# Chunked attention and a swish MLP on one core: blocks by batch, with crossbar and TensorE transposes, and the two products of a block in turn

## The chip, the cores and the metric

The kernel runs on one core of one Trainium2 chip. The metric is the device time of one execution in microseconds, as the median of several executions. Each run also lists the span of its instructions and the mean clock that the throttle granted to TensorE.

In this text PE is TensorE, PEld its weight loads, DVE is VectorE, ACT is ScalarE, POOL is GpSimd, and SP is SyncE, which here only issues DMAs.

## The reference

```python
def _attn_ref(q, k, v):                       # 8 batches, 8 heads, 576 tokens, 64 values each
    chunk, scale = 64, 1 / np.sqrt(64)        # attention inside chunks of 64 tokens only
    # q_c, k_c, v_c: reshaped to (B, H, 9, 64, 64)
    scores = scale * np.matmul(q_c, k_c.transpose(0, 1, 2, 4, 3))
    attn = softmax(scores)                    # cut
    return np.matmul(attn, v_c)               # reshaped back

def reference(q, k, v, w_in, w_out, beta):
    x = attn_out.transpose(0, 2, 1, 3).reshape(4608, 512)
    h = x @ w_in                              # 512 -> 2048, "first product"
    g = h * (1 / (1 + np.exp(-beta * h)))
    return g @ w_out                          # 2048 -> 512, "second product"
```

Both kernels compute in bf16 with f32 accumulation. They work on nine blocks of 512 tokens. A block has 64 matmuls of 128x512 in its first product and 64 in its second, 1152 "big" matmuls in all. Scores need q and k with the head dimension in the partitions, and the first product needs x with the model dimension in the partitions, so all three have to be transposed.

## The kernel before

Both kernels put every operation into the program order of its engine by a schedule of times, and waits on semaphores are worked out from what each operation reads and writes. This is also true of SP: in its program a DMA that has to wait stands before all DMAs scheduled later, even if those could go at once.

```python
def transpose_qk(blk, name, hp):              # 8 of these per block, 32x32 blocks, on VectorE
    P.op("dve", lambda e: e.transpose(
        tT[:, s, 4*hp:4*hp+4, :].rearrange("p g (t i) -> p i g t", i=4),
        ct[:, :, 2*hp:2*hp+2, :].rearrange("p i h d -> p i (h d)")), ...)

def scores(blk):                              # 128 matmuls of K=32, M=64, N=64
    ... e.matmul(A[64*hb:64*hb+64, m, col:col+64], kT[r, s, g, t], qT[r, s, g, t],
                 start=(dh == 0), stop=(dh == 1))

def transpose_x(blk, m, bank):                # 4 TensorE transposes, then a ScalarE copy
    ...
# ... loads, casts (POOL), exp (ACT), attend (PE), normalize (DVE) cut ...

for blk in range(NB):
    for n in range(16):                       # first product of blk beside second of blk - 1
        at(16 * blk + n, mm1, blk, n, bank)
        at(16 * (blk + 1) + n + 0.5, mm2, blk, n // 4, n % 4, 2 + (n // 4) % 2)
```

The softmax here doesn't subtract the row's maximum and nothing guards it: scores larger than these inputs give would overflow.

Of the kernel before, what the change touches and what calls it, by code (L numbers as in the profile page):

```python
# [6 lines left out]
ALU = mybir.AluOpType  # L7
# [9 lines left out]
class Program:  # L17
# [23 lines left out]
    def _depend(self, op, reads, writes):  # L41
# [17 lines left out]
        for key, v in writes:  # L59
            add(self.writer.get(key), op["queue"] == "pool")  # L60
            for r in self.readers.get(key, ()):
                add(r, False)
        for key, v in reads:
            self.readers.setdefault(key, []).append(op)
        for key, v in writes:
            self.writer[key] = op
            self.version[key] = v
            self.readers[key] = []
# [89 lines left out]
def bass_chunk_attention__then__act_swish_beta_kernel(nc, q, k, v, w_in, w_out, beta, out):  # L158
    B, H, S, D = q.shape
    NTOK = B * S  # L160
# [3 lines left out]
    NB = NTOK // 512  # L164
    CPB = S // 64

    with ExitStack() as es:
# [6 lines left out]
        beta_raw = sb("beta_raw", [128, NT], F32)  # L174
        beta_half = sb("beta_half", [128, NT], F32)
        w_in_bf = sb("w_in_bf", [128, NC, DFF], BF16)
        w_out_bf = sb("w_out_bf", [128, NT, 512], BF16)
        NWS = 4
        wstage = sb("wstage", [128, NWS, 2048], F32)
        NQS, NVS = 2, 2  # L180
        qstage = sb("qstage", [128, NQS, H, 256], F32)
        kstage = sb("kstage", [128, NQS, H, 256], F32)
        vstage = sb("vstage", [128, NVS, 4, 8, 64], F32)
        qcast = sb("qcast", [128, 4, H, 64], BF16)
        kcast = sb("kcast", [128, 4, H, 64], BF16)
        NQT = 2
        qT = sb("qT", [128, NQT, 2 * H, 128], BF16)
        kT = sb("kT", [128, NQT, 2 * H, 128], BF16)
        NVA = 2
        vaug = sb("vaug", [128, NVA, 8, 4, 66], BF16)  # L190
        E = sb("E", [128, 4, 512], BF16)
        rden = sb("rden", [128, 2, 2, 4], F32)
        x_sb = sb("x_sb", [128, 2, 512], BF16)
        NXT = 3
        xT = sb("xT", [128, NXT, NC, 512], BF16)
        tt = sb("tt", [128, 3, 512], BF16)
        g2 = sb("g2", [128, 2, NT, 512], BF16)
        NOS = 3
# [3 lines left out]
        F = es.enter_context(nc.psum_tensor("F", [128, 4, 512], F32))  # L202

        def chunk_runs(blk):
            g, end, runs = 8 * blk, 8 * blk + 8, []
            while g < end:
                b, c = divmod(g, CPB)
                n = min(end - g, CPB - c)
                runs.append((b, c, n, g - 8 * blk))
                g += n  # L210
            return runs


        def make_identity():
            P.op("pool", lambda e: e.memset(identity[:, :], 1.0), writes=[K("identity")])
            P.op("pool", lambda e: e.affine_select(
                out=identity[:, :], in_=identity[:, :], compare_op=ALU.is_equal, fill=0.0,
                base=0, pattern=[[-1, 128]], channel_multiplier=1),
                reads=[K("identity")], writes=[K("identity")])
            for s in range(NVA):  # L220
                P.op("pool", lambda e, s=s: e.memset(vaug[:, s, :, :, 64:65], 1.0),
                     writes=[K("vaug", s)])

        def load_beta():
            def f(e):
                with nc.allow_non_contiguous_dma(reason="beta is tiny"):
                    return e.dma_start(beta_raw[:, :], beta.rearrange("(t p) -> p t", p=128))
            P.dma("act", f, writes=[K("beta_raw")])
            P.op("dve", lambda e: e.tensor_single_scalar(
                beta_half[:, :], beta_raw[:, :], 0.5, ALU.mult),  # L230
# [3 lines left out]
        def load_qk(blk):  # L234
            s = blk % NQS
            for name, src, st in (("q", q, qstage), ("k", k, kstage)):
                for b, c, n, at in chunk_runs(blk):
                    def f(e, src=src, st=st, b=b, c=c, n=n, at=at):
                        a = src[b][:, 64 * c:64 * (c + n), :]
                        return e.dma_start(st[16 * at:16 * (at + n), s, :, :],  # L240
                                           a.rearrange("h (p i) d -> p h (i d)", i=4))
                    P.dma("sp", f, writes=[K(name + "stage", s, at, v=blk)])

        def load_v(blk):
            s = blk % NVS
            for b, c, n, at in chunk_runs(blk):
                for h in range(H):
                    def f(e, b=b, c=c, n=n, at=at, h=h):
                        a = v[b, h][64 * c:64 * (c + n), :]
                        r = 64 * (h % 2)  # L250
                        return e.dma_start(vstage[r:r + 64, s, h // 2, at:at + n, :],  # L251
                                           a.rearrange("(c j) d -> j c d", j=64))
                    P.dma("sp", f, writes=[K("vstage", s, at, h, v=blk)])

        def load_w_in(j):
            s = j % NWS

            def f(e):
                a = w_in[:, 512 * j:512 * (j + 1)].rearrange("(c p) f -> p c f", p=128)
                return e.dma_start(wstage[:, s, :].rearrange("p (c f) -> p c f", c=4), a)  # L260
            P.dma("sp", f, writes=[K("wstage", s, v=j)])

        def load_w_out(j):
            s = (4 + j) % NWS

            def f(e):
                a = w_out[512 * j:512 * (j + 1), :].rearrange("(t p) d -> p t d", p=128)
                return e.dma_start(wstage[:, s, :].rearrange("p (t d) -> p t d", t=4), a)
            P.dma("sp", f, writes=[K("wstage", s, v=4 + j)])

        def cast_w_in(j, engines):
            s = j % NWS
            for c, eng in enumerate(engines):
                dst = w_in_bf[:, c, 512 * j:512 * (j + 1)]
                src = wstage[:, s, 512 * c:512 * (c + 1)]
                if eng == "act":
                    P.op("act", lambda e, d=dst, a=src: e.activation(d, a, AF.Copy),  # L277
                         reads=[K("wstage", s, v=j)], writes=[K("w_in", j, c)])
                else:
                    P.op(eng, lambda e, d=dst, a=src: e.tensor_copy(d, a),  # L280
                         reads=[K("wstage", s, v=j)], writes=[K("w_in", j, c)])

        def cast_w_out(j, engines):
            s = (4 + j) % NWS
            for i, eng in enumerate(engines):
                dst = w_out_bf[:, 4 * j + i, :]
                src = wstage[:, s, 512 * i:512 * (i + 1)]
                if eng == "act":
                    P.op("act", lambda e, d=dst, a=src: e.activation(d, a, AF.Copy, scale=0.5),
                         reads=[K("wstage", s, v=4 + j)], writes=[K("w_out", 4 * j + i)])  # L290
                else:
                    P.op(eng, lambda e, d=dst, a=src: e.tensor_single_scalar(d, a, 0.5, ALU.mult),  # L292
                         reads=[K("wstage", s, v=4 + j)], writes=[K("w_out", 4 * j + i)])


        def stage_keys(name, blk):
            s = blk % NQS
            return [K(name + "stage", s, at, v=blk) for _, _, _, at in chunk_runs(blk)]

        def cast_qk(blk, name, eng):  # L300
            st, ct = (qstage, qcast) if name == "q" else (kstage, kcast)
            s = blk % NQS
            P.op(eng, lambda e: e.tensor_copy(  # L303
                ct[:, :, :, :].rearrange("p i h d -> p h i d"),
                st[:, s, :, :].rearrange("p h (i d) -> p h i d", i=4)),
                reads=stage_keys(name, blk), writes=[K(name + "cast", v=blk)])

        def transpose_qk(blk, name, hp):
            ct, tT = (qcast, qT) if name == "q" else (kcast, kT)
            s = blk % NQT  # L310
            P.op("dve", lambda e: e.transpose(  # L311
                tT[:, s, 4 * hp:4 * hp + 4, :].rearrange("p g (t i) -> p i g t", i=4),
                ct[:, :, 2 * hp:2 * hp + 2, :].rearrange("p i h d -> p i (h d)")),
                reads=[K(name + "cast", v=blk)], writes=[K(name + "T", s, hp, v=blk)])

        def cast_v(blk, eng, hp):
            s, sa = blk % NVS, blk % NVA
            keys = [K("vstage", s, at, h, v=blk) for _, _, _, at in chunk_runs(blk)
                    for h in (2 * hp, 2 * hp + 1)]
            P.op(eng, lambda e: e.tensor_copy(vaug[:, sa, :, hp, 0:64], vstage[:, s, hp, :, :]),  # L320
                 reads=keys, writes=[K("vaug", sa, hp, v=blk)])

        def scores(blk):
            s = blk % NQT
            for c2 in range(2):
                for hp in range(4):
                    for dh in range(2):
# [186 lines left out]
```

## Time and profile before

| | before |
|---|---|
| time, first median | 417.93 us |
| span of the profiled execution | 412.8 us |
| mean granted clock | 0.897 |
| steady block | about 41 us |
| big matmuls of a block at full clock, 128 x 216 ns | 27.6 us |

From the page of the kernel before come busy time and share of PE, its busy tenths in 40 slices, the granted clock in tenths in the same slices, and the shares of engines in the chain of work that ended last:

```profile
PE 309.5 (75%) x2988; PEld 149.7 (36%) x3024; DVE 217.8 (53%) x305; ACT 163.1 (40%) x261; POOL 64.4 (16%) x70
...
PE   0063486249993999399939993999299939999996
...
PEclk9998599569996899689968998899789969999999
...
PE 61%; DVE 22%; DMA 7%; SPq 5%; ACT 2%; issue 2%; POOL 1%; POOLq 0%
```

PE's slices fall to 2 or 3 once in about four slices, and the clock falls with them.

The chain of waits of the kernel before, in one stretch; the columns are start in us, length in us, and what the chain passed through:

```profile
205.10 1.23 DVE qT L311
206.33 1.14 DVE kT L311
...
213.74 1.15 DVE kT L311
214.93 2.14 PE A L336 x69
...
246.46 1.24 DVE qT L311
```

Eight stream transposes of 1.1 to 1.2 us stand in a row before the scores (line 336), and the next block begins 41.4 us later with the same. Who waited for whom (total us, times, longest):

```profile
PE A L336 <- DVE kT L311: 77.8, 34, 14.0
```

This is the hole in PE. The stretches just after one hole show what it does to the clock. The columns are stretch, length, busy time of PE, PEld, DVE, ACT and POOL, then granted clock, DMA share and GB/s:

```profile
173.00:176.00 3.00, 2.51 (x81) 2.29 (x83) 0.62 (x2) 0.00 (x0) 3.00 (x3) 0.50 0.25 44
176.00:179.00 3.00, 3.00 (x9) 1.13 (x8) 0.00 (x0) 0.13 (x1) 2.00 (x4) 0.54 1.08 321
```

PE is busy in the second stretch, but at half clock.

### The profile page before, as it was taken

The page shows a single profiled execution, that of the slowest core. Times are in us where ns is not written, and L with a number is a line of the kernel's source. Part 1 is how long each engine was busy: PE and PEld are TensorE (multiplying, and loading weights), DVE is VectorE, ACT ScalarE, POOL GpSimd, SP SyncE. Part 2 cuts the span into 40 slices and gives each one's busy share as a digit, 9 for nine tenths or more (in the row PEclk, how much of TensorE's full clock was granted, in tenths as well). Part 3 has the DMA queues.
Part 4 walks back from the last instruction along what each step waited for, and adds up shares of the span by engine and source line. Part 5 has one row for each costly group of instructions (what it writes and reads, how often), then busy time and mean ns, then how long its engine had stood idle before and what let it go on. Part 6 is the DMA issues. An engine that isn't in the chain of part 4 may idle for free.

```text
span 412.8 us, 7035 instructions
## 1 busy us (share of the span) xinstructions
PE 309.5 (75%) x2988; PEld 149.7 (36%) x3024; DVE 217.8 (53%) x305; ACT 163.1 (40%) x261; POOL 64.4 (16%) x70
## 2 busy tenths in 40 slices
PE   0063486249993999399939993999299939999996
PEld 0041332034442444244424442444144414444442
DVE  0934675575466346824682568246834673444320
ACT  1033086016550555055505550555055505554521
POOL 3407100754004100320022002300220000000000
PEclk9998599569996899689968998899789969999999
DMA  8998539897997932093209200001000100010111
GB/s 242 328 293 177 186 109 272 168 213 185 209 215 157 232 105 78 5 245 87 62 12 280 79 37 16 27 25 41 13 25 27 51 3 25 27 51 27 52 51 76
DMA packets 69358, 46.59 MB, mean 113 GB/s; under 512 B 42192, under 2 KB 60624, under 8 KB 69328
## 3 DMA queue, kind: packets, MB, share of 16 engines
q1 hardware_dynamic: 62080, 36.71, 35.9%
q10 hardware_dynamic: 7248, 9.45, 6.3%
q8 instruction: 23, 0.38, 0.4%
q14 instruction: 7, 0.06, 0.0%
HBM read 36.71 MB, written 9.44 MB: 112 GB/s over the span
## 4 chain that ended last, share of the span: by engine, by line
PE 61%; DVE 22%; DMA 7%; SPq 5%; ACT 2%; issue 2%; POOL 1%; POOLq 0%
PE F L403 28%; PE F L388 26%; DVE kT L311 9%; DVE qT L311 9%; DMA kstage<-in_k_dram 7%; PE A L336 4%; DVE g L396 3%; SPq L251 2%; SPq L240 2%; PE A L355 2%; PE A L378 2%; ACT tt L393 1%; POOL kcast L303 1%; DVE w_out_bf L292 1%; SPq L260 1%
## 5 line engine op out<-in xcount | busy, mean ns | idle before, releaser
L396 DVE SCALAR_TENSOR_TENSOR g<-tt,F 128x512 bf16<-128x512 bf16 x144 | 99.2, 690 | 148.7 <-ACT tt L393 148.7
L393 ACT ACTIVATE tt<-F,beta_half 128x512 bf16<-128x512 f32 x144 | 99.0, 688 | 189.0 <-PE F L388 183.3
L403 PE MATMUL F<-w_out_bf,g 128*128 128x512 bf16 x546 | 147.3, 393 | 15.1 <-POOL w_out_bf L292 10.6
L388 PE MATMUL F<-xT,w_in_bf 128*128 128x512 bf16 x570 | 154.0, 396 | 2.0 <-ACT w_in_bf L277 1.2
L403 PEld LDWEIGHTS F<-w_out_bf,g 128*128 128x128 bf16 x576 | 55.6, 100 | 78.3 <-DVE kT L311 11.0
L336 PE MATMUL A<-qT,kT 32*64 32x64 bf16 x1152 | 24.9, 232 | 77.8 <-DVE kT L311 77.8
L388 PEld LDWEIGHTS F<-xT,w_in_bf 128*128 128x128 bf16 x576 | 55.9, 102 | 66.3 <-issue 13.4
L303 POOL CAST qcast<-qstage 128x2048 bf16<-128x2048 f32 x9 | 17.1, 1895 | 222.0 <-DVE qT L311 174.7
L336 PEld LDWEIGHTS A<-qT,kT 32*64 32x64 bf16 x1152 | 20.5, 127 | 85.7 <-DVE kT L311 84.9
L311 DVE STREAM_TRANSPOSE kT<-kcast 128x512 bf16<-128x512 bf16 x36 | 47.6, 1323 | 5.8 <-POOL kcast L303 5.8
L311 DVE STREAM_TRANSPOSE qT<-qcast 128x512 bf16<-128x512 bf16 x36 | 47.2, 1311 | 6.5 <-POOL qcast L303 6.5
L344 ACT ACTIVATE E<-A 128x512 bf16<-128x512 f32 x36 | 20.4, 599 | 23.9 <-PE A L336 21.0
L408 ACT ACTIVATE ostage<-F 128x512 f32<-128x512 f32 x36 | 21.5, 597 | 19.6 <-PE F L403 19.6
L381 ACT ACTIVATE xT<-A 128x512 bf16<-128x512 bf16 x36 | 21.4, 595 | 13.3 <-PE A L378 13.3
L366 DVE TENSOR_TENSOR x_sb<-A,rden 128x512 bf16<-128x512 f32 x36 | 24.9, 691 | 1.2
L320 POOL CAST vaug<-vstage 128x512 bf16<-128x512 f32 x36 | 21.9, 642 | 2.9 <-DMA vstage<-in_v_dram 2.9
L303 POOL CAST kcast<-kstage 128x2048 bf16<-128x2048 f32 x9 | 17.1, 1896 | 9.1 <-DMA kstage<-in_k_dram 9.1
L378 PE MATMUL A<-identity,x_sb 128*128 128x128 bf16 x144 | 14.8, 229 | 3.2 <-DVE x_sb L366 3.2
L378 PEld LDWEIGHTS A<-identity,x_sb 128*128 128x128 bf16 x144 | 10.9, 101 | 12.4 <-DVE x_sb L366 5.8
L355 PE MATMUL A<-vaug,E 64*64 64x65 bf16 x576 | 12.8, 203 | 2.1 <-ACT E L344 1.6
L355 PEld LDWEIGHTS A<-vaug,E 64*64 64x64 bf16 x576 | 8.3, 111 | 16.6 <-issue 11.4
L364 DVE RECIPROCAL rden<-A 128x8 f32<-128x8 f32 x36 | 7.3, 201 | 6.2 <-PE A L355 6.1
(15 smaller groups left out, 25.4 us busy)
## 6 DMA issues: line engine op xcount, KB each, us to landing
out_dram<-ostage ACTq DMA_DIRECT2D x36, 256.0 KB, 2.0
wstage<-in_moe_w_in_dram SPq DMA_DIRECT2D x4, 1024.0 KB, 9.1
wstage<-in_moe_w_out_dram SPq DMA_DIRECT2D x4, 1024.0 KB, 6.7
qstage<-in_q_dram SPq DMA_DIRECT2D x2, 1024.0 KB, 5.4
kstage<-in_k_dram SPq DMA_DIRECT2D x2, 1024.0 KB, 8.5
vstage<-in_v_dram SPq DMA_DIRECT2D x16, 128.0 KB, 4.6
qstage<-in_q_dram SPq DMA_DIRECT2D x2, 896.0 KB, 10.4
kstage<-in_k_dram SPq DMA_DIRECT2D x2, 896.0 KB, 12.3
```

The costliest lines, as they stand in the source:

```text
L303: P.op(eng, lambda e: e.tensor_copy(ct[:, :, :, :].rearrange("p i h d -> p h i d"), st[:, s, :, :].rearrange("p h (i d) -> p h i d", i=4)) ...
L311: P.op("dve", lambda e: e.transpose(tT[:, s, 4 * hp:4 * hp + 4, :].rearrange("p g (t i) -> p i g t", i=4), ct[:, :, 2 * hp:2 * hp + 2, :]. ...
L320: P.op(eng, lambda e: e.tensor_copy(vaug[:, sa, :, hp, 0:64], vstage[:, s, hp, :, :]), reads=keys, writes=[K("vaug", sa, hp, v=blk)])
L336: return e.matmul(A[64 * hb:64 * hb + 64, m, col:col + 64], kT[r, s, g, t], qT[r, s, g, t], start=(dh == 0), stop=(dh == 1))
L355: return e.matmul(A[64 * c2:64 * c2 + 64, bank + hb, 128 * hp:128 * hp + 65], E[r, m, col:col + 64], vaug[r, sa, 2 * m + c2, hp, 0:65])
L366: P.op("dve", lambda e: e.tensor_tensor(x_sb[:, s, :].rearrange("p (h b d) -> p b h d", h=4, b=2), o[:, :, :, 0:64], rden[:, s, :, :].unsq ...
L378: P.op("pe", lambda e, hp=hp: e.transpose(dst[:, hp, :], x_sb[:, s, 128 * hp:128 * hp + 128], identity[:, :]), reads=[K("x", s, v=(blk, m) ...
L388: P.op("pe", lambda e, c=c: e.matmul(F[:, bank, :], w_in_bf[:, c, 128 * t:128 * t + 128], xT[:, sx, c, :], start=(c == 0), stop=(c == NC - ...
L393: P.op("act", lambda e: e.activation(tt[:, T % 3, :], F[:, bank, :], AF.Tanh, scale=beta_half[:, t:t + 1]), reads=[K("F", bank, v=("h", T) ...
L396: P.op("dve", lambda e: e.scalar_tensor_tensor(g2[:, sg, t, :], tt[:, T % 3, :], 1.0, F[:, bank, :], ALU.add, ALU.mult), reads=[K("F", ban ...
L403: P.op("pe", lambda e, t=t: e.matmul(F[:, bank, :], g2[:, sg, t, 128 * s:128 * s + 128], w_out_bf[:, t, :], start=(t == 0), stop=(t == NT ...
L408: P.op("act", lambda e: e.activation(ostage[:, N % NOS, :], F[:, bank, :], AF.Copy), reads=[K("F", bank, v=("o", N))], writes=[K("o", N % ...
```

## The change

The intent: free VectorE and the critical path of the q and k transposes, use one PE tile shape for scores and AV, cut the scores from 128 matmuls to 64, and let the first product of a block run before its second, with the next block's attention inside the second. Blocks are now the first 512 tokens of each batch, and the ninth block is the remaining 64 tokens of all batches. Blocks 0 and 1 transpose q and k on TensorE, and block 0 also x. All other transposes are done by DMA through the crossbar, issued by SP.

```diff
-        def transpose_qk(blk, name, hp):
-            P.op("dve", lambda e: e.transpose(...))
+        def turn_qk(blk, name):
+            P.dma("sp", lambda e: e.dma_start_transpose(
+                turned[name][:, :, :].rearrange("p h (m t) -> p (h m) t", m=4), cast[name][:, :]), ...)
+        def turn_x(blk, m):
+            P.dma("sp", lambda e: e.dma_start_transpose(
+                xT[:, blk % 2, :, 128 * m:128 * m + 128], x_sb[:, m, :]), ...)
+        def load(blk, name, m):      # 128 tokens x 8 heads: 1024 pieces of 256 bytes
+            P.dma("sp", ...)
 # ... blocks 0 and 1 (1024-byte loads, TensorE transposes), scores, attend cut ...
+        def load_beta():
+            P.dma("sp", f, writes=[K("beta_raw")])
+            P.op("dve", lambda e: e.tensor_single_scalar(
+                beta_half[:, :, :], beta_raw[:, :, :], 0.5, ALU.mult), ...)
+        def attention(blk, T):
+            at(T + 0.6, scores, blk, 0)                  # ... exp cut
+            for u in range(2):
+                for m in (2 * u, 2 * u + 1):
+                    at(T + 4.6 + 4 * u, attend, blk, m)
+                    at(T + 4.7 + 4 * u, normalize, blk, m)
+                    at(T + 4.8 + 4 * u, turn_x, blk, m)
+        def prepare(blk, T):
+            for i, name in enumerate("qkv"):
+                for m in range(4):
+                    at(T - 27 + 4 * i + m, load, blk, name, m)
+                    ...                                   # casts on POOL
+                        if m == 3:
+                            at(T - 10 + 4 * i, turn_qk, blk, name)
+        for blk in range(2, NB):
+            prepare(blk, 32 * blk - 16)
+            attention(blk, 32 * blk - 16)
         for blk in range(NB):
             for n in range(16):
-                at(16 * blk + n, mm1, blk, n, bank)
-                at(16 * (blk + 1) + n + 0.5, mm2, blk, n // 4, n % 4, 2 + (n // 4) % 2)
+                at(32 * blk + n, mm1, blk, n)
+                at(32 * blk + 16 + n, mm2, blk, s, part)
```

## The prediction

> **What bounds it now.** The page gives PE 75% busy; the chain of waits is PE 61%, DVE 22%, DMA 7%.
> 1. Head. In the chain the first MLP matmul starts at 50.1 us, after q and k loads and DVE transposes; the second block's kcast waits for DMA until 76.0.
> 2. Steady blocks. In the chain the first transpose of a block comes at 205.1, 246.5, 287.6, 328.1 us: about 41 us a block. A block has 128 big matmuls; the last stretch ran 40 in 8.63 us, 216 ns each, so 27.6 us are MLP. Before each block's scores eight DVE stream transposes (1.13 to 1.24 us each, 9.4 us) lie on the chain; the waits view has PE waiting 77.8 us in total for them. In each such hole the granted clock falls to 0.5 and stays there into the next matmuls (windows 173-176 us: 0.50, 176-179: 0.54, then 1.00). The Trainium skill, "TensorE: Matmul & The Clock Gate", Part 1, says that an idle window of about 3.4 us halves the clock; this trace agrees. That costs some 2 to 3 us more per block.
> 3. A tail of matmuls at clock 1.0 and a 3 us store.
>
> **What changes.** Removed: all 72 stream transposes (95 us of DVE), 32 of 36 x transpose groups from PE with their copies (595 ns each), half of the score matmuls (64 of K=64 per block, not 128 of K=32). Added: crossbar transposes of q, k (blocks 2 to 8) and x (1 to 8), 1.5 MB per block; q, k and v loads there in 256-byte packets. Order: 64 first-product matmuls, then 64 second-product with the next block's attention in them, over four F banks. ACT and DVE need 16 x 0.69 = 11 us in a first-product phase, PE 13.8, so PE remains the limit.
>
> **DMA.** In a window (193-198 us) with only v loads 2543 packets took 54.6% of 16 engines' 5 us, 17 ns each; 12288 per block are 13 us, stores 3. The crossbar is the unknown: no record here has one. The skill, "DMA: Bandwidth & Descriptors", Latency and other measured facts, gives 261 GB/s: estimate 6 us per block; at a third of that rate DMA would approach the block's time. I expect it to fit, with about 1 us of waits per block.
>
> **Sum (estimates from these durations).**
> - First MLP matmul at 24 us instead of 50: half-size loads, PE transposes, casts shared out.
> - Block 0 ends, w_out arriving at DMA pace (some 7 us of stalls), at 64.
> - Blocks 1 to 7: 27.65 + scores 0.9 + AV 1.2 (16 now cost about 0.3) + waits 1.2 = 31 us each: 217.
> - Block 8: 27.65 us, tail 3.
> - Span 312; timed runs lie 5 us above the span (417.9 against 412.8): 317, rounded to 318.
>
> So about 100 us go: 25 in the head, 70 in steady blocks, 5 elsewhere. The removed stream transposes were nearly all on the critical path; the ACT savings weren't.
>
> **Signs.** Right: no DVE in the chain beyond the head; clock 1.0 from about 60 us on; a block in 30 to 32 us; big matmuls 216 ns apart; first MLP matmul between 20 and 28 us. Wrong: PE waiting for qT, kT or xT by several us per block, with dips of the clock; SP's queue full of transpose issues; DMA share near 100% in steady blocks; stride-2 weight loads slowing the first product.
>
> **What would make it wrong.** Crossbar transposes much slower than estimated, or queued behind the 256-byte loads: 350 to 420 us. A smoother head and no waits: about 300.
>
> Predicted 318 us, 8 in 10 between 301 and 350. Chances: faster by over 2% 0.95; within 2% 0.02; slower 0.03.

## More of the kernel before

One more view is needed later, PE's own order of work near the start (start us, us, operation, and in brackets the idle time before it and what ended it):

```profile
32.47 3.13 PE L388 MATMUL F<-xT,w_in_bf 128*128 128x512 bf16 x7 [1.21 <-ACT w_in_bf L277]
...
47.67 2.14 PE L336 MATMUL A<-qT,kT 32*64 32x64 bf16 x80 [1.94 <-DVE kT L311]
50.14 3.71 PE L388 MATMUL F<-xT,w_in_bf 128*128 128x512 bf16 x11 [0.33 <-issue]
```

The first big matmuls ran at 32.47 us. Only 8 belong to that group in program order (the trace has 7 records of them), then PE stood behind the scores of the second block until 50.14.

## The result, and the profile after

The changed kernel took 359.05 us (356.19 to 360.6, four runs), the kernel before 417.58 us (415.41 to 418.06). The ratio is 0.861, with a 95% interval of 0.857 to 0.866. A ratio here is the one that the measuring program gives for the fast runs of both kernels; it is not quite the quotient of the medians, which is 0.860. The change is 14% faster. The prediction was 24% and its range ended at 350 us.

From the page of the changed kernel, the same lines as before:

```profile
PE 293.9 (83%) x2384; PEld 137.9 (39%) x2384; DVE 149.6 (42%) x237; ACT 153.5 (43%) x228; POOL 73.6 (21%) x112
...
PE   0047998729996999799979995999499959999995
...
PEclk9999999958998999899989996999789989999999
...
PE 62%; SPq 17%; DMA 9%; DVE 8%; issue 2%; ACT 1%
```

DVE went from 22% to 8% of the chain. In its place came SPq, the issuing of DMAs by SP (17% after 5%), and a little more DMA (9% after 7%). PE's slices and the clock still dip once in each block. One block of the chain of waits of the changed kernel:

```profile
100.53 0.70 DVE x_sb L375
101.23 0.37 SPq L381
...
102.95 0.58 SPq L283
...
106.67 5.55 DMA xT<-x_sb
112.22 0.79 issue
113.01 15.66 PE F L399 x64
```

Read it downwards. The x of the second token group is ready at 101.23. SP issues its transpose and then the q loads (line 283) until 106.6, although VectorE's timeline has the third group's x ready at 104.6. Only then comes the third x transpose, which lands 5.55 us after the start of its issue. The fourth is behind it, and the first product (line 399) starts at 113.01. The waits view:

```profile
PE F L399 <- DMA xT<-x_sb: 25.1, 6, 8.6
```

Its total of six waits includes one of 8.6 us for block 1. SP's own waits, in the same form:

```profile
SPq L381 <- DVE x_sb L375: 86.7, 9, 16.8
```

So SP, too, waits for x, and it waits 86.7 us. What that holds up is seen in SP's order for one block:

```profile
100.41 2.50 SPq L381 DMA_TRANSPOSE xT<-x_sb  x2
102.95 3.67 SPq L283 DMA_DIRECT2D qstage<-in_q_dram  x4
106.67 3.18 SPq L381 DMA_TRANSPOSE xT<-x_sb  x2
109.89 4.36 SPq L283 DMA_DIRECT2D kstage<-in_k_dram  x4
114.30 5.99 SPq L283 DMA_DIRECT2D vstage<-in_v_dram  x4
120.33 3.65 SPq L298 DMA_TRANSPOSE qT<-qcast  x1
124.02 1.43 SPq L298 DMA_TRANSPOSE kT<-kcast  x1
```

The clock after the hole, in the same columns as before:

```profile
113.00:116.00 3.00, 2.99 (x8) 1.09 (x9) 0.39 (x1) 0.69 (x1) 0.86 (x2) 0.51 1.27 265
116.00:119.00 3.00, 3.00 (x14) 1.31 (x13) 1.68 (x3) 2.02 (x3) 0.98 (x2) 0.92 1.11 184
```

The half clock lasts into the next matmuls as it did before. The first products of blocks 1 to 7 took 15.2 to 16.7 us instead of 14.0.

The head has a hole of its own. From the timeline of the changed kernel:

```profile
6.25 1.04 POOL L259 CAST kcast<-kstage 128x1024 bf16<-128x1024 f32 x1 [4.68 <-DMA kstage<-in_k_dram]
...
11.76 0.74 SPq L225 DMA_DIRECT2D beta_raw<-in_moe_beta_dram  x1
...
16.37 0.89 DVE L228 TENSOR_SCALAR beta_half<-beta_raw 128x16 f32<-128x16 f32 x1 [16.37 <-DMA beta_raw<-in_moe_beta_dram]
17.17 0.68 DVE L259 CAST qcast<-qstage 128x1024 bf16<-128x1024 f32 x1
...
34.80 1.47 PE L399 MATMUL F<-xT,w_in_bf 128*128 128x512 bf16 x6 [0.52 <-DVE xT L259]
```

POOL cast k at 6.25, so q, issued before k, had very probably landed too (the first experiment below bears this out). VectorE cast q only at 17.17, because its first instruction in program order was the halving of beta, and beta's load had been issued at 11.76, behind the v loads.

The starts of the first products of blocks 0 to 8, from PE's timeline, give the terms of the predicted sum (the measured ones add up to the 356.2 us of the profiled execution, the fastest of the four):

| term | predicted us | measured us | difference |
|---|---|---|---|
| first MLP matmul | 24 | 34.8 | +10.8 |
| block 0, until block 1's first product | 40 | 42.9 | +2.9 |
| blocks 1 to 7 | 217 | 244.9 | +27.9 |
| block 8 and the tail | 31 | 31.9 | +0.9 |
| timed run less span | 5 | 1.7 | -3.3 |

Where did the 58 us of gain come from? The program order gives the number of big matmuls ahead of each block's scores. With about 330 done the kernel before stood at 173.2 us (332 matmuls, at the last group of block 4's scores) and the changed one at 129.5 (324, block 3's scores), so 43.6 us were won up to there. The next 512 big matmuls, four steady blocks, took 164.7 and 142.3 us: 22.4 us won, 5.6 per block where 10 were predicted. In the last stretch 7.8 us were given back: from these points on the changed kernel still has 8 more big matmuls to do than the kernel before, and one more block boundary with its hole.

### The profile page after: what moved, and what is told of

Its sections match the earlier page's. It is cut to its first block, busy times and chain, and to the rows that moved or that the text cites. A ratio compares the mean times of both kernels' runs of the same rounds, so it can differ in the third digit from the quotient of the medians.

```text
span 354.5 us, 5695 instructions
## 1 busy us (share of the span) xinstructions
PE 293.9 (83%) x2384; PEld 137.9 (39%) x2384; DVE 149.6 (42%) x237; ACT 153.5 (43%) x228; POOL 73.6 (21%) x112
## 4 chain that ended last, share of the span: by engine, by line
PE 62%; SPq 17%; DMA 9%; DVE 8%; issue 2%; ACT 1%
PE F L399 39%; PE F L414 18%; SPq L283 10%; DMA xT<-x_sb 8%; SPq L381 6%; DVE x_sb L375 3%; DVE kT L259 3%; PE A L348 2%; PE A L365 2%; DMA beta_raw<-in_moe_beta_dram 1%; PE F L327 1%; DVE qcast L259 1%; DVE rden L373 1%; SPq L311 1%; PE F L389 1%
## 5 line engine op out<-in xcount | busy, mean ns | idle before, releaser
L399 PE MATMUL F<-xT,w_in_bf 128*128 128x512 bf16 x576 | 139.8, 408 | 29.9 <-DMA xT<-x_sb 25.1
L414 PE MATMUL F<-w_out_bf,g 128*128 128x512 bf16 x576 | 130.3, 379 | 0.0
L399 PEld LDWEIGHTS F<-xT,w_in_bf 128*128 128x128 bf16 x576 | 59.1, 104 | 110.2 <-issue 51.1
L259 POOL CAST qcast<-qstage 128x512 bf16<-128x512 f32 x28 | 17.2, 614 | 134.1 <-DMA qstage<-in_q_dram 134.1
L259 POOL CAST kcast<-kstage 128x512 bf16<-128x512 f32 (+1 forms) x31 | 20.3, 655 | 35.7 <-DMA kstage<-in_k_dram 35.7
L365 PEld LDWEIGHTS A<-vaug,E 64*64 64x64 bf16 x576 | 11.7, 112 | 8.4 <-issue 4.3
L256 ACT ACTIVATE qT<-F 128x1024 bf16<-128x1024 bf16 x2 | 4.9, 2442 | 19.6 <-PE F L327 19.6
L261 POOL TENSOR_SCALAR w_out_bf<-wstage 128x512 bf16<-128x512 f32 (+1 forms) x5 | 9.5, 1910 | 15.2 <-DMA wstage<-in_moe_w_out_dram 15.2
L348 PE MATMUL A<-qT,kT 64*64 64x64 bf16 x576 | 7.4, 199 | 4.0 <-DVE kT L259 3.9
L348 PEld LDWEIGHTS A<-qT,kT 64*64 64x64 bf16 x576 | 6.1, 112 | 7.9 <-DVE kT L259 4.6
```

Source lines behind the costliest of these rows:

```text
L259: P.op(eng, lambda e: e.tensor_copy(dst, src), reads=r, writes=wr)
L348: return e.matmul(A[64 * c2:64 * c2 + 64, bank, col:col + 64], turned["k"][r, hp, t], turned["q"][r, hp, t])
L365: return e.matmul(A[r, bank, 128 * (h % 4):128 * (h % 4) + 65], E[r, 2 * (m // 2) + h % 2, col:col + 64], vaug[r, m, h, 0:65])
L399: P.op("pe", lambda e, c=c: e.matmul(F[:, bank, :], w_in_bf[:, c, 256 * e0 + i:256 * e0 + 256:2], xT[:, blk % 2, c, :], start=(c == 0), st ...
L414: P.op("pe", lambda e, t=t: e.matmul(F[:, s, :], g2[:, t, 128 * s:128 * s + 128], w_out_bf[:, t, :], start=(t == 0), stop=(t == NT - 1)), ...
```

## The experiments

All outputs are right. The kernel before had medians of 416.7 to 417.0 us in these rounds.

### Head: the halving of beta later

```diff
             P.dma("sp", f, writes=[K("beta_raw")])
-            P.op("dve", lambda e: e.tensor_single_scalar(      # in load_beta
+        def halve_beta():
+            P.op("dve", lambda e: e.tensor_single_scalar(
         at(-87.9, load_beta)
+        at(-74.05, halve_beta)
```

> Only the halving of beta is moved in VectorE's program order, from its first place to just before the first product; nothing else changes. Theory head-of-line: in the changed kernel VectorE's first instruction waited until 16.37 us for the beta load, and the q cast, ready for its data from about 6 us on (the k cast on GpSimd started at 6.25), stood behind it. Expected: first q cast at 6 to 8 us, limited next by the last q/k load; first MLP matmul at 25 to 27 us instead of 34.8; span 6 to 9 us shorter (about 347). Rival, the head is bound by the loads themselves or by the 2.43 us PSUM copies: first MLP matmul not before 32 us, span within 3 us of 354.5.

Measured: 348.87 us (346.73 to 350.53), ratio 0.838; the first product starts at 23.9 us, earlier than the 25 to 27 expected. (The profiled execution was the slowest of the four, with a span of 348.8 us.) The first instruction of VectorE is now:

```profile
5.00 0.69 DVE L261 CAST qcast<-qstage 128x1024 bf16<-128x1024 f32 x1 [5.00 <-DMA qstage<-in_q_dram]
```

The rival falls. The loads and copies had allowed 23.9 us all along, which is the 24 us of the prediction. A single instruction of 0.9 us at the head of an in-order engine cost 10.9 us of the start. The Trainium skill, "TensorE: Matmul & The Clock Gate", its table of specifications, gives VectorE's queue as strict FIFO; this trace agrees.

### Block boundary: q loads after the x transposes

```diff
-                    at(T - 27 + 4 * i + m, load, blk, name, m)
+                    at(T - 23.1 + 0.02 * m if name == "q" else T - 27 + 4 * i + m, load, blk, name, m)
```

> Only the place of the four q loads of a block in SP's order changes: after all four crossbar transposes of x instead of between the second and third. Theory queue order: the third and fourth x transpose waited for the issue (3.7 to 5.4 us) and the data (1 MB) of the q loads. Expected: PE's wait for xT falls from 4 to 5 us per block to under 1 us, the clock stays at 1.0, blocks 2 to 6 take 31 to 32 us instead of 34 to 37, span 18 to 24 us shorter (about 333). Rival, the crossbar transposes are slow in themselves or the DMA engines (83% busy in steady blocks) are the limit: the wait shrinks by less than half, or turns into a wait for qT and kT before the scores; span at most 8 us shorter.

Measured: 369.69 us (368.63 to 370.35), ratio 0.887, so slower than the change by about 10.6 us. The wait for xT went as the theory of queue order said, except 7.2 us once, for block 1. But blocks 2 to 6 took 36.5 to 38.2 us, and PE now waits here:

```profile
PE A L348 <- DMA kT<-kcast: 33.7, 6, 7.6
```

In this narrow form the theory fell, and so did the expectation of 333 us. The rival had foreseen a wait for kT. SP's order shows a third explanation, though:

```profile
137.76 6.69 SPq L381 DMA_TRANSPOSE xT<-x_sb  x4
144.49 3.64 SPq L283 DMA_DIRECT2D qstage<-in_q_dram  x4
...
162.93 1.43 SPq L298 DMA_TRANSPOSE kT<-kcast  x1
```

SP is hardly ever idle from the first x transpose to the k transpose, 26.6 us, and the k transposes landed 4.4 us after their issue. Then come scores, AV and normalization, until the next x is ready, and SP can go on. This is a ring: x of a block, SP's orders for the next block, kT, scores, x of the next block. SP waits for x before it issues the loads, though the loads need nothing of x. In the changed kernel the same ring was nearly as long: kT landed at 128.4 (124.02 plus 4.4), and the scores began at 129.54. So in the changed kernel itself PE waited in the steady blocks for xT alone, with about 1 us to spare on the side of kT. Moving the q loads shifted the delay from one side of the ring to the other, and made the ring longer: SP no longer used its wait for the third group's x to issue q loads, so in the blocks shown kT landed 28.8 us after the second group's x was ready instead of 27.2, and after PE's wait for kT the half clock fell on the work that makes the next x (8.2 us from scores to x instead of 6.4). The Trainium skill, "DMA: Bandwidth & Descriptors", Anatomy of one DMA, in a section on DMAs issued by GpSimd, says that any semaphore wait happens on the issuing sequencer before dispatch; SP's 86.7 us of waiting for x agree for SP.

### Block boundary: x on TensorE

```diff
-                    at(T + 4.8 + 4 * u, turn_x, blk, m)
+                    at(T + 7 + 4.6 * u, turn_x_pe, blk, m, A, 2 * (m % 2), "act" if m % 2 == 0 else "dve")
-                at(28.9 + 2 * u, turn_x, 1, m)
+                at(29.6 + 2 * u, turn_x_pe, 1, m, A, 2 * (m % 2), "act" if m % 2 == 0 else "dve")
```

> All x transposes on TensorE again (blocks 1 to 8 as in block 0, into the free attention banks, copies shared by ScalarE and VectorE); q and k stay on the crossbar. Both theories of the block boundary expect the wait for xT to go: a block costs PE 4 x 0.22 us more, so 31 to 32.5 us per block, span 18 to 24 us shorter. If queue order alone is the cause, this equals the run with late q loads within 1%; if the crossbar's own latency or its share of the DMA time matters, this run is clearly faster than that one (by 5 us or more).

Measured: 321.65 us (321.13 to 322.61), ratio 0.773. Every block from 1 on takes 30.7 to 30.8 us, the clock is 1.0 throughout, and no wait for a crossbar transpose is left on PE. It is far faster than the run with late q loads. By the expectation this spoke for the crossbar's latency or its share of the DMA. But it also fits the ring, which was thought of only after these results, as SP no longer waits for x. Later runs tell these apart.

### Both single changes together

> Both single changes together (halving of beta later, q loads after the x transposes). If head and block boundary are separate causes, the two savings add up within 3 us: span about 354.5 minus 30, that is 322 to 330 us, about what was predicted for the changed kernel. If the earlier head only runs into the weight loads, the sum falls short by 5 us or more.

Measured: 359.81 us (357.45 to 360.24), ratio 0.863, against an expectation of 322 to 330. The premise of a saving from late q loads had failed. Set against that run, the beta edit again saved 9.9 us, so the head is a separate cause.

### The ring broken, the crossbar kept: loads a block ahead

```diff
-                    at(T - 27 + 4 * i + m, load, blk, name, m)
+                    at(T - 27 + 4 * i + m if blk == 2 else T - 37.9 + 0.8 * (4 * i + m), load, blk, name, m)
```

> As the changed kernel, x still on the crossbar; only SP's order changes: from block 3 on the twelve q, k and v loads of a block are put behind the q and k transposes of the block before, so ahead of that block's x transposes, not behind them. Theory loop on SP: x ready -> SP issues x transposes, next block's loads and q, k transposes in order -> kT -> scores -> attention -> x ready; this ring of dependences set the 34 to 37 us of a block, and the run with late q loads only moved the wait from xT (gone) to kT (5.5 us each). With loads a block ahead, a turn of the ring holds only six transposes: blocks 3 to 8 take 31 to 32 us, clock 1.0, span 330 to 338. Rival, DMA capacity: the same bytes and packets move, the DMA engines were 83% busy at 34 us a block, so blocks stay at 33.5 us or more and the span above 345.

Measured: 326.34 us (325.24 to 327.31), ratio 0.783; the span, 325.4 us, is shorter than the 330 to 338 expected. Blocks 1 to 8 started 29.9 to 31.8 us apart. SP's order now:

```profile
100.00 6.69 SPq L381 DMA_TRANSPOSE xT<-x_sb  x4
106.73 3.24 SPq L298 DMA_TRANSPOSE qT<-qcast  x1
110.02 3.33 SPq L298 DMA_TRANSPOSE kT<-kcast  x1
113.40 3.56 SPq L283 DMA_DIRECT2D qstage<-in_q_dram  x4
...
129.87 6.69 SPq L381 DMA_TRANSPOSE xT<-x_sb  x4
```

The loads (line 283) stand after the k transpose and before the next wait for x, and SP has time to spare. The transposes are not faster than before: four of x take 6.69 us to issue, as in the run with late q loads, and those of k land 5.6 us after the start of their issue in the median, where it was 4.4 in the changed kernel. One block in the table of stretches:

```profile
109.40:139.30 29.90, 29.58 (x254) 14.09 (x257) 14.41 (x24) 15.45 (x24) 7.20 (x12) 1.00 1.04 195
```

The clock is 1.00. The DMA share counts each packet's own time, so it can pass 1. DMA did move 195 GB/s here against 153 to 173 in the changed kernel's blocks 2 to 6. DMA capacity was therefore not what held the changed kernel at 34 to 37 us. It is close to being the next limit: PE still waited 11.9 us for xT, 7.9 of them once, at block 1, which this edit does not reach.

### The ring kept, nobody waiting for the crossbar's x

x goes through TensorE as above, and the crossbar transposes of x are issued as well, at their old places, into a tile that is never read:

```diff
-                xT[:, blk % 2, :, 128 * m:128 * m + 128], x_sb[:, m, :]),
+                spare[:, blk % 2, :, 128 * m:128 * m + 128], x_sb[:, m, :]),
+                    at(T + 4.8 + 4 * u, turn_x, blk, m)
                     at(T + 7 + 4.6 * u, turn_x_pe, blk, m, A, ...)
```

> As the run with x on TensorE (319.7 us span, 30.8 us a block), but the crossbar transposes of x are issued too, at their old places on SP, into a tile that nobody reads. Loop on SP: SP again waits for x before it goes on to loads and q, k transposes; from the old trace x ready to kT landed is 27.2 us, scores to x ready 6.4 us, so a block cannot be under about 33.6 us, with PE waiting for kT by some 2 to 3 us: span 333 to 345. Rival, crossbar latency (PE only suffered because it needed xT itself): nobody waits for these transposes, blocks stay at 31 to 31.5 us, span under 326.

Measured: 349.42 us (344.94 to 351.28; the longest was a slow run and is left out of the ratio, and the median of the three fast ones is 349.08), ratio 0.835. Blocks 2 to 7 took 33.6 to 38.1 us. PE's wait:

```profile
PE A L349 <- DMA kT<-kcast: 21.1, 6, 6.1
```

The span of the profiled execution, 347.9 us, is 3 us above the top of what was expected, because the estimate of the ring's length was short: blocks took 35.6 us in the mean, not 33.6. The direction is plain. Nothing needed the results of these transposes, and they cost 28 us against the run with x on TensorE.

### The same, with the ring broken

The unread transposes stay, and the loads go a block ahead (the two edits above together).

> The run with unread crossbar transposes of x (349.4 us, blocks of about 35 us, PE waiting some 3 us a block for kT) with one more edit: the loads of a block a block ahead in SP's order. Same bytes, same packets, same transposes, nobody waits for the x transposes. Loop on SP: the wait for kT goes, blocks return to 30.8 us, time within 4 us of the run with x on TensorE (321.7), that is 318 to 326 us. If instead the added crossbar traffic itself had slowed that run, it stays above 340.

Measured: 321.45 us (321.29 to 322.71), ratio 0.772, blocks of 30.7 to 30.8 us. With the same DMA work as the last run all 28 us are back. So the added traffic was harmless, and SP's order was the cause. Nor did the transposes of k land sooner once the loads stood elsewhere: their median from issue to landing was 5.8 us here and 4.4 in the run with the ring kept.

### Best version: x on TensorE, beta later

> x on TensorE and the halving of beta later, together. The head saving of the beta run was about 10 us in the timed runs (348.9 against 359); if it is independent of the block boundary, 321.7 minus 8 to 10: 312 to 314 us. If the earlier head runs into the weight and first-batch loads, 315 to 320.

Measured: 310.17 us (309.96 to 311.28), ratio 0.745, first product at 23.6 us, the following blocks 30.8 us each. The beta edit saved 11.5 us here, a little more than the 8 to 10 expected. The two causes add up.

### Order of the PSUM copies

```diff
-                 turned[...].rearrange("x h (p i) -> x h i p", i=4), mid.rearrange("x (h i p) -> x h i p", ...)
+                 turned[...].rearrange("x h (p i) -> x h p i", i=4), mid.rearrange("x (h i p) -> x h p i", ...)
```

> As the run before it, and the PSUM copies of q and k of blocks 0 and 1 run through the same elements in another order: destination contiguous, PSUM source strided, instead of destination with a step of 4 elements. The copies took 2.43 us on both engines, where 512-element copies with a contiguous destination took 0.60 (ScalarE) and 0.42 us (VectorE), so 1.2 and 0.85 us for 1024. If the strided bf16 destination is what doubled them, they fall to about 1.2 and 0.9 to 1.2 us, the head shortens by 2 to 3 us and the time by as much. If it is the 4-level access pattern or the strided side wherever it is, they stay at 2.4 us and nothing changes.

The groups view (line, engine, operation, output and input, count, then busy us and mean ns of one, then idle time before) of the changed kernel:

```profile
L256 ACT ACTIVATE qT<-F 128x1024 bf16<-128x1024 bf16 x2 | 4.9, 2442 | 19.6 <-PE F L327 19.6
L259 DVE COPY kT<-F 128x1024 bf16<-128x1024 bf16 x2 | 4.9, 2430 | 3.4 <-PE F L327 3.4
```

And of this run:

```profile
L258 ACT ACTIVATE qT<-F 128x1024 bf16<-128x1024 bf16 x2 | 2.0, 1024 | 8.3 <-PE F L329 8.3
L261 DVE COPY kT<-F 128x1024 bf16<-128x1024 bf16 x2 | 2.5, 1225 | 4.1 <-PE F L329 4.1
```

Both engines write the same elements to the same places. With the destination written in order the copies took 1.02 us on ScalarE and 1.23 on VectorE instead of 2.44 and 2.43. The time is 306.17 us (305.79 to 306.68), ratio 0.735, 4.0 us less than the run before it, where 2 to 3 were expected. This beats both kernels.

### All fixes, with the crossbar kept for x of blocks 2 to 8

Loads a block ahead, beta later, copy order, and x of block 1 alone on TensorE.

> All fixes with the crossbar kept for x of blocks 2 to 8: loads a block ahead, halving of beta later, copy order, and x of block 1 on TensorE, since its crossbar transposes cost PE 7.9 us behind the first loads. Against the 306.2 us version, a block costs PE 0.9 us less (29.9 instead of 30.8), so up to 6 us are to be had: 300 to 303 us if xT always lands in time. In the loads-ahead run PE still waited up to 1.5 us for xT in later blocks; if that grows with DMA at 89% busy, 304 to 310 us, and the version with all x on TensorE stays the best.

Measured: 308.59 us (306.02 to 309.99), ratio 0.739 with an interval of 0.735 to 0.744, against 0.733 to 0.737 for the version above. So nothing was gained. Blocks took 29.9 to 32.5 us, and PE waited 5.2 us for xT in all.

## Why the prediction was wrong

**Right.** The stream transposes, on the chain before every block's scores in the kernel before, are gone from the critical path, and the kernel is faster. (No run takes them out alone, so their share is not separated from that of the new order of the products.) PE is the limit again wherever nothing holds it up: with x on TensorE a block takes 30.8 us and with loads ahead 29.9 in the best case, where 31 had been predicted. The half clock after a hole was read correctly, but the idle window of about 3.4 us, which the prediction cites from the Trainium skill, does not fit all holes: PE's waits of 2.25 and 2.23 us before blocks 3 and 4 of the changed kernel were followed by a clock of 0.50, while after a wait of 2.42 us before block 2 of the last run above it stayed at 1.00. The worry "queued behind the 256-byte loads" named the right place, and the range given for it, 350 to 420 us, holds the measured time; but it was given as what would make the prediction wrong and not put into the sum.

**The step that failed** is "I expect it to fit, with about 1 us of waits per block". The argument compared DMA work with the block's time, as if throughput were the question. It did not follow SP's program order, which was to be had: loads of the next block stand behind transposes that wait for x of this one. Blocks 1 to 7 took 244.9 us. Seven blocks of 29.9 us, as the loads-ahead run's best, are 209.3; PE's waits for xT in these blocks are 16.5 us (25.1 less the 8.6 at block 1); one idle time put down to "issue" adds 4.3; and first products at partly half clock add 13.8 us over 14.0 each. That sums to 243.9. The run with unread transposes (ring kept, 349 us) and the one with the ring broken (321 us), with the same transfers, show that order and not capacity or latency was the cause.

**The second term that was mis-sized** is "First MLP matmul at 24 us". It came at 34.8. Without the wait for beta it came at 23.9, so the rest of the head fits the term; the prediction shows no working for it, so how far this was luck can't be told. The wait for beta on VectorE was overlooked, although it stood in the profile before, where VectorE waited 10.1 us for beta before its first transpose.

**A misreading** is "instead of 50". The chain lists only what lies on it. PE's own timeline shows the first big matmuls of the kernel before at 32.47 us. The changed kernel was thus not earlier at its first big matmul. It won in the start because PE did not stop so long after them. With 76 big matmuls done the kernel before stood at 89.0 us and the changed one at 52.9, which is 36 of the 43.6 us. In the kernel before PE stood behind the second block's scores until 50.1 us, then waited 10.6 us for a cast of w_out, then stood behind the third block's scores until 89.0.

**Two smaller terms.** The crossbar estimate of 6 us per block from the skill's 261 GB/s was somewhat low: while the k transpose of the last block ran with no other transfer (305.0 to 306.5 us), the DMA moved 215 GB/s, which would make 7 us for the 1.5 MB. From issue to landing such a transpose of 512 KB took 4.4 us, a latency that the sum had no term for. Neither decided the time, as the loads-ahead run shows. And 5 us between timed run and span was wrong: in one execution it is 1.7. The profiled execution and the timed ones of the kernel before had differed by the rest.

**Still open.** Blocks 4 to 6 of the changed kernel took 36 to 37 us, blocks 2 and 3 only 34. In the later ones the q loads took 5.1 to 6.2 us to issue instead of 3.7 (in the last of them they were eight smaller ones). Why was not tested. Nor was it tested whether larger packets for q and k would free the version with the crossbar from its last waits.

## What to carry to other kernels

A queue that issues DMAs in program order is an engine like any other. If an operation on it waits for a result of this block and the loads of the next block stand behind it, the loads join the ring of dependences of the loop, and the block takes the time of the ring even where every engine and the DMA have time to spare. Put loads a whole block ahead of any such wait, and look for the first instruction of each engine and ask what it waits for. A wait that moved from one operand to another when the order was changed was the sign of such a ring here.

## What the Trainium skill lacked or had wrong

- "DMA: Bandwidth & Descriptors", Latency and other measured facts: 261 GB/s for DMA transposes, from one kernel. Here the DMA moved 215 GB/s while one of 512 KB between SBUF tiles ran alone, and from issue to landing it took 4.4 us.
- The same page says where a semaphore wait of a DMA happens, but not what follows for a loop: loads behind a waiting transpose cost 28 us here (349.4 against 321.5 us, same transfers).
- The same page has sequencer cycles for transposes of other sizes, but no issue time for these on this chip: SP took 1.2 to 2.7 us for 128x512 and 1.4 to 4.4 us for 128x2048 in the changed kernel.
- "VectorE: DVE Perf Modes" and "ScalarE: Activation LUTs" have no figure for bf16 copies out of PSUM into a destination with a step of 4 elements: 2.43 and 2.44 us for 128x1024, against 1.23 and 1.02 us with the destination in order. Other pages treat strided access to SBUF, but none has a figure for this copy.
- "VectorE: DVE Perf Modes", The three transpose paths, gives 390 ns for a TensorE transpose of 128x128, and no figure for a stream of them. Here 16 of them cost a block about 0.9 us in all (30.8 against 29.9 us).
